# The leftover rows of four batches as one more seven-product half batch, and a new order of all steps

## Chip, cores, metric

One NeuronCore of a Trainium2 chip runs the whole kernel; the other cores are idle. The metric is the device time of one execution in microseconds, taken as the median of three timed runs.

## What is computed

Packed attention followed by a feed-forward block, all float32. With batch 8, 8 heads, 576 tokens, head width 64, and 32 packed queries per head:

```python
p_packed = sm_attn(p, k, v)
out = sm_attn(q, p_packed, p_packed)
...
h = x @ w_in
g = h * (1.0 / (1.0 + np.exp(-h)))
return (g @ w_out).astype(np.float32)
```

`x` is the attention output of all 4608 tokens with the heads side by side (512 wide); `w_in` is 512 x 2048, `w_out` 2048 x 512. `sm_attn` is a softmax attention with the scale 1/8.

## The kernel before

Precision: each big product of float32 values is made of three products of rounded parts, upper by upper, upper by lower and lower by upper (`todo` in `terms`, lines 669 to 675). An upper half is a cast on ScalarE, a lower half a subtraction on VectorE.

Work is done batch by batch. The attention of a batch ends in weights of the packed tokens (`a2`), and `w_in` is multiplied into the packed tokens once per batch (`Packs`, steps `pp`, `pu`, `pl`), a quarter of the 2048 hidden features at a time. A *unit* then makes hidden values for some features of a batch and multiplies them with `w_out`:

- Batches 0 and 1 (the early units 0 to 31): step `h` makes one block of 128 features for all 576 tokens in `ps_two` (line 615), `g` and `l` the SiLU and its halves, `o` the products with `w_out` into `ps_acc` (line 673, 12 matmuls of 512 columns). Meanwhile `w_in` and `w_out`, which arrive as float64, are converted by ScalarE, VectorE and GpSimd (steps `wf` to `wl`), and sums of `w_out` blocks are made and kept in DRAM (`r`, `R`, `ru`, `rl`, `rk`, `T`).
- Batches 2 to 7: a unit is a half batch (256 of its 288 tokens, `MAIN`) and a pair of feature blocks. `B` makes the hidden values (12 matmuls of 288 columns), `G` their SiLU into tile `g`, `I` three sums on GpSimd (`pair_sums`, lines 644 to 649), `F` and `L` the upper and lower halves of seven 128 x 128 blocks (lines 657 to 667), `O` the products (`pair_products`, lines 716 to 737): Strassen's form with seven block products in place of eight, 21 matmuls of 256 columns into four accumulators. Three of the seven need sums of `w_out` blocks, which `S` loads for each unit from DRAM (768 KB). After 8 pairs `E` (`pair_rows`) adds the accumulators up and stores a half batch.
- Each half batch leaves 32 tokens, 64 per batch. `N` puts their SiLU values into the tile `rest`. For two batches at a time these 128 rows are a *rest* unit of four feature blocks: `F`, `L` on 512 columns of `rest`, and `O` is `rest_products` (lines 705 to 712), 12 matmuls of 512 columns in the plain form. There are 16 rest units: 32 to 35 (batches 0 and 1), 68 to 71, 104 to 107 and 140 to 143, the last of the kernel. `Y` (`rest_rows`) stores them.

Between early and later units stand `Z0.` and `Z1.`: they give the memory of `win` (all of `w_in`) and of the early accumulators to others. From then on a quarter of `w_in` is fetched from DRAM (`pf`, 1024 KB, into the single buffer `w_quarter`) before its `pp`.

The order on TensorE, VectorE, ScalarE and SyncE is the order of the steps in the table `ORDER`, as written; only GpSimd's is left to the scheduler. SyncE issues nearly all DMAs, in that order, and a DMA that waits holds those behind it. `g`, `g_hi` and `g_lo` have two buffers each, `ps_two` two, the four accumulators one.

Of the kernel before, what the change touches and what calls it, by code (L numbers as in the profile page):

```python
# [66 lines left out]
pl5 aH1.1 aL1.1 o6 o7 e7.0 h8 g8 r0 e7.1 wf14 l8 wc12 h9 as2.1 o8 g9 ws13 ac2.1 h10 am2 wz12 h11 l9 g10 wc13 v2 pp6 R0
wi12 wj12 wf15 l10 ru0 rl0 wz13 o9 o10 rk0 r1 R1 ax2.0 ax2.1 g11 l11 pu6 at2.0 o11 q2 pl6 h12 h14 wi13 ws14 g12 h13
at2.1 wc14 ws15 wj13 wf17 l12 o12 T0 wz14 ay2 wi14 g13 l13 o13 wc15 wz15 wi15 g14 l14 pp7 h15 ru1 rl1 pu7 pl7 wj14 r2
wj15 wu15 wl15 o14 h16 g15 ws17 l15 wf16 h17 wc17 rk1 g16 wz17 l16 wu14 wl14 o15 e15.0 g17 e15.1 wi17 wj17 wf18 h18  # L70
l17 o16 ws16 wc16 ar2 R2 wz16 wi16 h19 g18 l18 o17 wj16 pp8 ru2 rl2 g19 l19 aa2 pu8 r3 o18 ws18 pl8 b0 an2 wc18 h20
o19 wz18 ai2 wi18 g20 l20 wj18 wu18 h21 wf19 ws19 aj2 R3 rk2 wl18 wc19 wz19 wi19 wj19 g21 pp9 pu9 l21 pl9 o20 x2 h22
g22 l22 o21 wu19 wl19 h23 aS2.1 ru3 rl3 o22 x3 g23 aT2.1 l23 T1 r4 R4 rk3 x0 X0 X1 x1 aM2.1 aN2.1 h24 X0 T3 o23 g24
l24 h25 h26 e23.0 ru4 rl4 rk4 e23.1 g25 l25 r5 o24 pp10 g26 l26 aS2.0 o25 aT2.0 pu10 pl10 aX2.1 h27 aM2.0 aN2.0 aX2.0
aD2.0 X1 b1 aE2.0 T2 h28 k3 o26 R5 ru5 rl5 rk5 T5 g27 l27 h29 T4 aV2.0 aH2.0 g28 r6 R6 l28 o27 g29 l29 o28 h31 aD2.1
aL2.0 h30 ru6 rl6 rk6 T6 r7 o29 g30 R7 l30 aE2.1 aV2.1 v3 g31 o30 aH2.1 ru7 X0 l31 rl7 o31 rk7 e31.0 e31.1 pp11 Z0.
# [870 lines left out]
```

## Time and profile before

| | us |
|---|---|
| median of 3 runs | 680.04 (679.95 to 680.74) |
| profiled execution, its own time | 681.22 |
| its span | 679.4 |
| TensorE busy in the span | 660.8 |
| VectorE busy | 428.9 |
| ScalarE busy | 423.3 |
| GpSimd busy | 229.1 |

Times in the profile count from the start of the span; what lies around the span (681.22 - 679.4 = 1.8 us) is not in it. A matmul's row shows its latency, so that busy time of TensorE covers short gaps; the pace of a run of matmuls is the length of that run over its count. The granted clock was 1.0 of 2.4 GHz all along after the first microseconds.

### The profile page before, as it was taken

What the parts mean: (1) busy time and instruction counts of PE and PEld (TensorE: products, weight loads), DVE (VectorE), ACT (ScalarE), POOL (GpSimd) and SP (SyncE); (2) the same over time, 40 slices, a digit from 0 to 9 for tenths busy, and PEclk for the clock granted to TensorE, in tenths of its full rate; (3) what the DMA queues carried; (4) which work ended last, traced back from release to release, by engine and by line L of the source; (5) the groups of instructions that cost most, each with busy time, mean ns of one, the idle gap of its engine ahead of it and who ended that gap; (6) DMA issues with size and microseconds to landing.
All of it is one profiled execution on the core that took longest, in us unless ns stands there. A gap on an engine that the chain in (4) does not pass through costs nothing.

```text
span 679.4 us, 14828 instructions
## 1 busy us (share of the span) xinstructions
PE 660.8 (97%) x5980; PEld 584.2 (86%) x5980; DVE 428.9 (63%) x595; ACT 423.3 (62%) x706; POOL 229.1 (34%) x337
## 2 busy tenths in 40 slices
PE   8898999999999999999999999999999999999997
PEld 6676778787878998899888998899988999899995
DVE  4999999987784356653576428763567426663433
ACT  4798876757557456764466638684367644766442
POOL 1111213243222543444242533445341343444440
PEclk9999999999999999999999999999999999999999
DMA  9748284968688669877798477977889278767441
GB/s 360 321 158 332 71 325 121 335 232 328 241 317 311 226 264 371 330 291 268 269 354 312 132 293 274 368 272 270 325 299 363 81 263 302 247 251 259 166 171 46
DMA packets 55107, 178.62 MB, mean 263 GB/s; under 512 B 21760, under 2 KB 25856, under 8 KB 47360
## 3 DMA queue, kind: packets, MB, share of 16 engines
q1 hardware_dynamic: 54944, 177.56, 70.9%
q8 instruction: 47, 0.77, 0.4%
q10 hardware_dynamic: 96, 0.13, 0.1%
q14 instruction: 20, 0.16, 0.1%
HBM read 149.42 MB, written 24.12 MB: 255 GB/s over the span
## 4 chain that ended last, share of the span: by engine, by line
PE 72%; DVE 9%; ACT 8%; DMA 4%; issue 4%; SPq 2%; POOL 1%; ACTq 0%; DVEq 0%; POOLq 0%
PE ps_acc L673 42%; PE ps_two L615 23%; PE ps_two L304 6%; DMA win<-in_w_out 2%; DVE g_lo L633 2%; SPq L388 2%; DMA sums_of_w<-sums_of_w 1%; ACT g_hi L663 1%; DVE g_lo L667 1%; DVE o L815 1%; PE ps_two L408 1%; ACT g L626 1%; DMA w_raw<-in_w_out 1%; ACT L188 1%; ACT g_hi L627 1%
## 5 line engine op out<-in xcount | busy, mean ns | idle before, releaser
L667 DVE TENSOR_TENSOR g_lo<-g,g_hi 128x896 fp32r<-128x896 f32 x96 | 108.5, 1134 | 132.5 <-ACT g_hi L663 129.7
L673 PE MATMUL ps_acc<-wo_hi,g_hi 128*128 128x256 f32 (+1 forms) x576 | 183.0, 318 | 0.7 <-DVE o L815 0.7
L673 PE MATMUL ps_acc<-wo_hi,g_lo 128*128 128x256 f32 (+1 forms) x576 | 182.1, 316 | 0.7 <-DVE g_lo L633 0.6
L673 PE MATMUL ps_acc<-wo_lo,g_hi 128*128 128x256 f32 (+1 forms) x576 | 181.4, 315 | 0.0
L615 PE MATMUL ps_two<-a_hi,pw_hi 128*128 128x288 f32 x512 | 152.0, 297 | 0.8 <-ACT tm L331 0.3
L615 PE MATMUL ps_two<-a_hi,pw_lo 128*128 128x288 f32 x512 | 150.9, 295 | 0.0
L615 PE MATMUL ps_two<-a_lo,pw_hi 128*128 128x288 f32 x512 | 150.6, 294 | 0.2 <-DVE a_lo L546 0.2
L647 POOL TENSOR_TENSOR g<-g 128x128 f32<-128x128 f32 x96 | 51.8, 540 | 273.1 <-ACT g L637 241.1
L663 ACT CAST g_hi<-g 128x896 fp32r<-128x896 f32 x96 | 90.0, 941 | 77.0 <-POOL g L649 40.6
L673 PEld LDWEIGHTS ps_acc<-wo_hi,g_hi 128*128 128x128 f32 x576 | 108.2, 188 | 14.8 <-issue 6.9
L673 PEld LDWEIGHTS ps_acc<-wo_hi,g_lo 128*128 128x128 f32 x576 | 108.3, 188 | 10.2 <-DVE g_lo L633 2.4
L673 PE MATMUL ps_acc<-sums_of_w,g_hi 128*128 128x256 f32 x576 | 115.6, 282 | 1.0 <-DMA sums_of_w<-sums_of_w 1.0
L673 PEld LDWEIGHTS ps_acc<-wo_lo,g_hi 128*128 128x128 f32 x576 | 108.2, 188 | 6.6 <-DVE wo_lo L297 0.3
L615 PEld LDWEIGHTS ps_two<-a_hi,pw_hi 128*128 128x128 f32 x512 | 96.3, 188 | 7.1 <-issue 3.0
L673 PEld LDWEIGHTS ps_acc<-sums_of_w,g_hi 128*128 128x128 f32 x576 | 87.8, 188 | 15.0 <-issue 13.3
L615 PEld LDWEIGHTS ps_two<-a_lo,pw_hi 128*128 128x128 f32 x512 | 96.4, 188 | 1.4 <-DVE a_lo L546 0.4
L615 PEld LDWEIGHTS ps_two<-a_hi,pw_lo 128*128 128x128 f32 x512 | 96.2, 188 | 0.0
L637 ACT ACTIVATE g<-ps_two 128x512 f32<-128x512 f32 x96 | 57.1, 598 | 42.9 <-PE ps_two L615 22.7
L673 PE MATMUL ps_acc<-sums_of_w,g_lo 128*128 128x256 f32 x288 | 80.0, 278 | 0.0
L648 POOL TENSOR_TENSOR g<-g 128x256 f32<-128x256 f32 x96 | 73.1, 763 | 6.5
L649 POOL TENSOR_TENSOR g<-g 128x128 f32<-128x128 f32 x96 | 56.7, 592 | 6.5
L673 PEld LDWEIGHTS ps_acc<-sums_of_w,g_lo 128*128 128x128 f32 x288 | 54.2, 188 | 0.4 <-DVE g_lo L667 0.4
(131 smaller groups left out, 838.1 us busy)
## 6 DMA issues: line engine op xcount, KB each, us to landing
sums_of_w<-sums_of_w SPq DMA_DIRECT2D x96, 768.0 KB, 6.4
w_quarter<-w_in SPq DMA_DIRECT2D x22, 1024.0 KB, 7.2
kvq_t<-in_v SPq DMA_DIRECT2D x8, 1280.0 KB, 9.3
kvq_t<-in_pkT SPq DMA_DIRECT2D x7, 1216.0 KB, 10.4
out<-o SPq DMA_DIRECT2D x16, 512.0 KB, 3.6
kvq_t<-in_qT SPq DMA_DIRECT2D x7, 1152.0 KB, 8.4
w_raw<-in_w_in SPq DMA_DIRECT2D x6, 1024.0 KB, 8.1
sums_of_w<-w_sums SPq DMA_DIRECT2D x8, 768.0 KB, 4.6
```

The costliest lines, as they stand in the source:

```text
L188: nc.scalar.activation(ready, ident[:, :1], (AF.Exp, AF.Silu)[n])
L304: nc.tensor.matmul(bank(par)[NP * i : NP * i + NP], lhs(r, i), rhs(r, i), start=True, stop=True)
L388: nc.sync.dma_start(self.e1T[NP * at : NP * at + NP, : some.shape[1], i], some)
L615: nc.tensor.matmul(bank, p[:, par, cols], a[:, par], start=(n == 0), stop=(n == len(todo) - 1))
L633: nc.vector.tensor_tensor(g_lo[:, c], g[:, c], g_hi[:, c].bitcast(F32), ALU.subtract)
L637: nc.scalar.activation(g[:, : 4 * P].rearrange("p (e s) -> p e s", e=2), made["h", u, None][..., :MAIN], AF.Silu)
L647: nc.gpsimd.tensor_tensor(x[:, 4], x[:, 0], x[:, 2], ALU.subtract)
L648: nc.gpsimd.tensor_tensor(x[:, 5:7], x[:, 0:5:4], one, ALU.subtract)
L649: nc.gpsimd.tensor_tensor(x[:, 7], x[:, 3], x[:, 6], ALU.add)
L663: nc.scalar.copy(both[0], g)
L667: nc.vector.tensor_tensor(g_lo, g, g_hi.bitcast(F32), ALU.subtract)
L673: nc.tensor.matmul(out, g[:, rows], w, start=(first and n == 0), stop=(last and n == 2), skip_group_check=True)
```

## The change

The rest rows of batches 0 to 3, and again of 4 to 7, become 256 rows, a further half batch with eight pair units. `rest` holds two batches; those of the first two are written to DRAM (`D`, `kept_rest`) and read back (`C`, `load_rest`) into a buffer of `kvq`, and `M` (`copy_rest`) puts both together in a tile `g` with two ScalarE copies. `I`, `F`, `L`, `O` then follow as for any pair; in the last eight units `I` runs on VectorE. Rest units are now 64 to 71 and 136 to 143, with no `B`, `G` or `N`. The pairs of every second half batch are taken as 4 to 7, 0 to 3, so that four tiles of sums stay from one half to the next: `S` falls from 96 to 76. The last unit puts its bank-2 products last, and the stores of the last rest half are eight DMAs, four on each of two queues, in place of four.

```diff
-PACKS += [(b, j * FJ, FJ) for b in range(EARLY, B) for j in range(NJ)]
+PACKS += [(b, j * FJ, FJ) for b in range(EARLY, B) for j in ((0, 1, 2, 3), (2, 3, 0, 1))[b % 2]]
+PAIRS = (0, 1, 2, 3, 4, 5, 6, 7), (4, 5, 6, 7, 0, 1, 2, 3)
...
-L40 B42 G42 X1 O39 S40 O40 N41 F41 N42 ay3.1 B43 N43 I42 F42 L41 S41 aa3 G43 O41 X0 an3 L42 ai3 aj3 B44 S42 N44 G44
...
+ay3.1 F38 L38 B40 N40 G40 B41 aa3 N41 I39 an3 S38 F39 L39 G41 T6 O38 S39 T7 ai3 B42 q3 I40 aj3 O39 pf15 F40 L40 G42 I41
...
-    units += [(0, f, "rest") for f in range(0, NF, FJ)]
     for b in range(EARLY, B):
-        units += [(b, (hf, p)) for hf in range(2) for p in range(NPAIR)]
-        if b % 2:
-            units += [(b - 1, f, "rest") for f in range(0, NF, FJ)]
+        units += [(b, (hf, p)) for hf in range(2) for p in PAIRS[(b + hf) % 2]]
+        if b % 4 == 3:
+            units += [(b - 3, ("rest", p)) for p in PAIRS[1]]
...
-        nc.gpsimd.tensor_tensor(x[:, 4], x[:, 0], x[:, 2], ALU.subtract)
-        nc.gpsimd.tensor_tensor(x[:, 5:7], x[:, 0:5:4], one, ALU.subtract)
-        nc.gpsimd.tensor_tensor(x[:, 7], x[:, 3], x[:, 6], ALU.add)
+        engine = nc.vector if units[u][0] == B - 4 and units[u][1][0] == "rest" else nc.gpsimd
+        engine.tensor_tensor(x[:, 4], x[:, 0], x[:, 2], ALU.subtract)
+        engine.tensor_tensor(x[:, 5:7], x[:, 0:5:4], one, ALU.subtract)
+        engine.tensor_tensor(x[:, 7], x[:, 3], x[:, 6], ALU.add)
+
+    def keep_rest(j):
+        nc.sync.dma_start(kept_rest[j], rest[:, FJ * j : FJ * j + FJ].rearrange("p f e h s -> p (f e h s)"))
+
+    def load_rest(n):
+        t = in_turn(kvq, [P, 5 * DM], F32, "kvq_t")[:, : NF * P]
+        nc.sync.dma_start(t.rearrange("p (j x) -> p j x", j=NJ), kept_rest.rearrange("j p x -> p j x"))
+        made["rest", n] = t.rearrange("p (f s) -> p f s", s=P)
+
+    def copy_rest(u):
+        b, (_, p) = units[u]
+        g = hidden[u] = in_turn(gp_main, [P, 8 * P], F32, "g")
+        g = g[:, : 4 * P].rearrange("p (e r s) -> p r e s", e=2, r=2)
+        nc.scalar.copy(g[:, 0], made["rest", b // 4][:, 2 * p : 2 * p + 2])
+        nc.scalar.copy(g[:, 1], rest[:, 2 * p : 2 * p + 2].rearrange("p f e h s -> p f (e h s)"))
...
-    def rest_products(u):
...
-        x = summed_tiles.pop((b, hf, p))
+        x = summed_tiles[p]
...
-        term(2, low, 6, *w(f2, high))
+        if not final:
+            term(2, low, 6, *w(f2, high))
         term(3, low, 1, *t(1))
         term(3, high, 3, *w(f1, high))
+        if final:
+            term(2, low, 6, *w(f2, high))
...
-        x = summed_tiles[b, hf, p] = in_turn(tp, [P, 2, 3 * HALF], F32R, "sums_of_w", TP_BUFS)
+        x = summed_tiles[p] = tp.tile([P, 2, 3 * HALF], F32R, name="sums_of_w", tag=f"sums_of_w_{p % TP_BUFS}", bufs=1)
...
+    def rest_rows(n):
+        o = pair_rows(n, "rest", n == 1)
+        for k in range(2):
+            for m in range(4):
+                at = (4 * n + 2 * k) * S + m * HS + MAIN
+                (nc.scalar if n and m % 2 else nc.sync).dma_start(out[at : at + REST], o[m * REST : m * REST + REST, k])
```

Three places of the new order follow, as rows of one engine each (line, operation, tile written <- tiles read, size, count).

SyncE, where early units end and the rest begins; `out` are the stores of the last early half batches. Before:

```order
L794 DMA out<-o 128x2x512 x2
L556 DMA w_quarter<-w_in_114 128x2048
L744 DMA sums_of_w<-sums_of_w 128x1536
L777 DMA wo_hi<-first_sums 128x256
L777 DMA wo_lo<-first_sums 128x256
L744 DMA sums_of_w<-sums_of_w 128x1536 x3
L556 DMA w_quarter<-w_in_114 128x2048
```

Now:

```order
L653 DMA kept_rest<-rest 128x512
L783 DMA wo_hi<-first_sums 128x256
L783 DMA wo_lo<-first_sums 128x256
L799 DMA out<-o 128x2x512 x2
L558 DMA w_quarter<-w_in_115 128x2048
L750 DMA sums_of_w<-sums_of_w 128x1536 x3
L558 DMA w_quarter<-w_in_115 128x2048
```

The first quarter (`pf13`) still stands right behind the two stores.

TensorE at the same place, from the last matmul of the early `o31` to the first `pp` on a fetched quarter (`pp13`); the rows between, left out, are the further matmuls of the same kinds. Before:

```order
L673 MATMUL ps_acc<-wo_hi,g_lo 128x512
L304 MATMUL ps_two<-win,ppT 32x512 x16
L673 MATMUL ps_acc_2221<-wo_hi,g_hi 128x512
...
L304 MATMUL ps_two<-kvq_t 32x288 x16
...
L615 MATMUL ps_two<-a_hi,pw_hi 128x288
...
L304 MATMUL ps_two<-w_quarter,ppT 32x512 x8
```

Now:

```order
L684 MATMUL ps_acc<-wo_hi,g_lo 128x512
L306 MATMUL ps_two<-kvq_t 32x288 x8
L306 MATMUL ps_two<-win,ppT 32x512 x8
L615 MATMUL ps_two<-a_hi,pw_hi 128x288
...
L306 MATMUL ps_two<-kvq_t 32x288 x8
L306 MATMUL ps_two<-w_quarter,ppT 32x512 x8
```

Before, three rest units (`O32` to `O34`) and two `B` stand between; now only `as3.0`, `pp12`, `B32`, `B33` and `as3.1`.

VectorE from the last main units into the last rest units; `o<-ps_acc` are the five additions of `E7.1`. Before:

```order
L667 TENSOR_TENSOR g_lo<-g,g_hi 128x896 x7
L667 TENSOR_TENSOR g_lo<-rest,g_hi 128x512
L815 TENSOR_TENSOR o<-ps_acc_2222,o 128x2x256
L815 TENSOR_TENSOR o<-ps_acc_2221,o 128x256
L815 TENSOR_TENSOR o<-ps_acc_2224,o 128x256
L815 TENSOR_TENSOR o<-ps_acc_2223,o 128x256
L815 TENSOR_TENSOR o<-ps_acc_2224,o 128x512
L667 TENSOR_TENSOR g_lo<-rest,g_hi 128x512 x3
```

Now:

```order
L648 TENSOR_TENSOR g<-g 128x128
L649 TENSOR_TENSOR g<-g 128x256
L650 TENSOR_TENSOR g<-g 128x128
L678 TENSOR_TENSOR g_lo<-g,g_hi 128x896
L806 TENSOR_TENSOR o<-ps_acc_2280,o 128x2x256
L806 TENSOR_TENSOR o<-ps_acc_2279,o 128x256
L806 TENSOR_TENSOR o<-ps_acc_2282,o 128x256
L806 TENSOR_TENSOR o<-ps_acc_2281,o 128x256
L806 TENSOR_TENSOR o<-ps_acc_2282,o 128x512
L678 TENSOR_TENSOR g_lo<-g,g_hi 128x896
```

Two `I` (136 and 137) and `L136` now stand ahead of the five additions, and of each later unit VectorE gets three sums and a lower half of 896 columns.

## Rows read from the trace of the kernel before

**Rows 1.** The page's busy times of the engines over the span.
```profile
PE 660.8 (97%) x5980; PEld 584.2 (86%) x5980; DVE 428.9 (63%) x595; ACT 423.3 (62%) x706; POOL 229.1 (34%) x337
```

**Rows 2.** Busy time by stretch: PE, PEld, DVE, ACT, POOL, clock, DMA share, GB/s.
```profile
20.00:140.00 120.00, 112.05 (x944) 88.06 (x943) 113.81 (x161) 94.65 (x162) 29.61 (x24) 1.00 0.65 236
195.00:217.00 22.00, 22.00 (x176) 16.13 (x176) 13.85 (x18) 13.71 (x22) 3.27 (x6) 1.00 0.98 371
217.00:660.00 443.00, 440.38 (x4223) 408.33 (x4223) 241.88 (x329) 262.62 (x435) 176.51 (x282) 1.00 0.74 270
```

**Rows 3.** What TensorE waited for: us in total, times, longest.
```profile
PE ps_acc L673 <- DMA sums_of_w<-sums_of_w: 1.0, 1, 1.0
```

**Rows 4.** The chain that ended last, in order of time: start us, us, what.
```profile
187.70 8.19 PE ps_acc L673 x36
195.89 1.88 PE ps_two L304 x32
...
290.75 4.78 PE ps_acc L673 x42
...
488.88 6.34 PE ps_two L615 x48
...
518.98 10.90 PE ps_acc L673 x48
```

**Rows 5.** Timeline of SyncE's DMA issues at 195 to 200: start us, us.
```profile
196.05 1.88 SPq L794 DMA_DIRECT2D out<-o  x2
197.98 1.17 SPq L556 DMA_DIRECT2D w_quarter<-w_in  x1
```

**Rows 6.** The tile w_quarter: its 22 loads, from issue to landing.
```profile
DMA to landing us min/median/max: 4.7/7.2/11.7
```

**Rows 7.** Timeline of TensorE at 195.5 to 212: scores, and the first fetched quarter.
```profile
200.64 1.20 PE L304 MATMUL ps_two<-kvq_t 64*32 64x288 f32 x32
210.60 1.09 PE L304 MATMUL ps_two<-w_quarter,ppT 64*32 64x512 f32 x16
```

**Rows 8.** Groups by form: line, engine, op, tiles, shapes, count | busy, mean ns | idle before.
```profile
L667 DVE TENSOR_TENSOR g_lo<-g,g_hi 128x896 fp32r<-128x896 f32 x96 | 108.5, 1134 | 132.5 <-ACT g_hi L663 129.7 <-PE ps_two L615 2.5
L663 ACT CAST g_hi<-g 128x896 fp32r<-128x896 f32 x96 | 90.0, 941 | 77.0 <-POOL g L649 40.6 <-PE ps_acc L673 35.1 <-DVE tm L364 0.7
L581 DVE TENSOR_TENSOR pw_lo<-ps_two,pw_hi 128x1024 fp32r<-128x1024 f32 x31 | 37.6, 1215 | 22.8 <-ACT pw_hi L578 22.4
L578 ACT CAST pw_hi<-ps_two 128x1024 fp32r<-128x1024 f32 x31 | 31.4, 1017 | 18.5 <-PE ps_two L304 18.5
L667 DVE TENSOR_TENSOR g_lo<-rest,g_hi 128x512 fp32r<-128x512 f32 x16 | 10.9, 683 | 10.3 <-ACT g_hi L663 10.3
L816 ACT COPY o<-ps_acc 128x256 f32<-128x256 f32 x12 | 4.5, 371 | 8.6 <-PE ps_acc L673 8.6
L800 DVE TENSOR_TENSOR o<-o 128x256 f32<-128x256 f32 x4 | 1.6, 412 | 3.5 <-ACT o L799 3.5
```

**Rows 9.** Timeline at 655 to 680, around the last `E` and the first last rest unit.
```profile
662.14 0.28 PE L673 MATMUL ps_acc<-sums_of_w,g_lo 128*128 128x256 f32 x1
...
662.46 0.37 ACT L816 COPY o<-ps_acc 128x256 f32<-128x256 f32 x1 [0.91 <-PE ps_acc L673]
...
662.87 2.60 DVE L815 TENSOR_TENSOR o<-ps_acc,o 128x512 f32<-128x512 f32 x5 [0.59 <-ACT o L816]
...
663.20 0.28 PE L673 MATMUL ps_acc<-wo_hi,g_lo 128*128 128x256 f32 x1
...
664.23 0.47 PE L673 MATMUL ps_acc<-wo_hi,g_hi 128*128 128x512 f32 x1 [0.75 <-DVE o L815]
```

**Rows 10.** Timeline at 674.9 to 679.4, the end.
```profile
675.03 0.39 PE L673 MATMUL ps_acc<-wo_hi,g_lo 128*128 128x512 f32 x1
675.46 0.69 DVE L801 TENSOR_TENSOR o<-ps_acc,o 128x512 f32<-128x512 f32 x1 [0.31 <-PE ps_acc L673]
676.18 0.81 SPq L808 DMA_DIRECT2D out<-o  x2
676.18 0.87 ACTq L808 DMA_DIRECT2D out<-o  x2
```

More of the change, by code (lines that the diff above doesn't have):

```diff
@@ L67 @@
[L67 to L76, printed above, removed]
@@ new lines @@
+e31.0 ac3.0 e31.1 pp12 pu12 pl12 B32 N32 Z0. G32 I32 B33 Z1. pf13 N33 as3.1 ac3.1 G33 S34 F32 L32 pp13 pu13 pl13 B34
+I33 F33 L33 N34 S32 B35 S33 pf14 O32 G34 I34 B36 am3 ax3.0 ax3.1 ar3 F34 O33 at3.0 at3.1 N36 L34 S35 S36 O34 N35 G35
+G36 pp14 I35 F35 pu14 B37 L35 G37 I36 O35 F36 ay3.0 X1 N37 pl14 I37 B38 F37 L36 N38 S37 B39 G38 N39 L37 O36 O37 G39 I38
+ay3.1 F38 L38 B40 N40 G40 B41 aa3 N41 I39 an3 S38 F39 L39 G41 T6 O38 S39 T7 ai3 B42 q3 I40 aj3 O39 pf15 F40 L40 G42 I41
+E2.0 B43 F41 L41 N42 O40 I42 N43 aS3.0 aT3.0 G43 aM3.0 pp15 I43 F42 aS3.1 pf16 pu15 aT3.1 O41 pl15 L42 aM3.1 B44 k4 F43
@@ new lines @@
+G127 I127 S127 I126 aL7.1 F126 L126 B129 S126 O125 F127 B128 N128 N129 G128 I128 O126 L127 O127 G129 E7.0 B130 F128
+L128 G130 B131 I129 I130 N130 O128 F129 L129 G131 I131 F130 B133 N133 N131 O129 B132 F131 L130 O130 L131 G132 I132 N132
+S132 G133 I133 F132 L132 O131 B134 B135 F133 L133 G134 O132 S133 O133 N135 G135 S134 I134 X1 I135 F134 L134 F135 L135
+O134 M136 I136 M137 I137 F136 L136 S135 O135 E7.1 N134 M138 F137 L137 O136 M139 I138 I139 O137 F138 L138 F139 L139 O138
+M140 I140 F140 S140 L140 M141 I141 S141 M142 I142 O139 F141 L141 O140 O141 F142 L142 M143 I143 S142 X0 S143 F143 L143
@@ L123 @@
+O142 O143 Y1
 """
@@ L703, in packed_attention_ffn @@
     low, high = slice(0, HALF), slice(HALF, DM)
-    def rest_products(u):
-        b, f, _ = units[u]
-        first, last = f == 0, f + FJ == NF
-        for n in sorted(range(FJ), key=lambda n: n % 2) if last else range(FJ):
-            bank = 0 if n % 2 == 0 and (f + n) // 2 in summed else 2
-            begun = opened.get(("rest", b, bank))
-            opened["rest", b, bank] = True
-            products(acc[bank], u, f + n, n, not begun, last and n >= FJ - 2)
     opened = {}
@@ L718, in pair_products @@
         g_hi, g_lo = hidden[u][-2:]
-        last = p == NPAIR - 1
+        last = is_last(u)
+        final = last and u == len(units) - 1
         def term(bank, cols, at, w_hi, w_lo):
-            key = "pair", b, hf, bank
+            key = b, hf, bank
             begun = opened.get(key)
@@ L794, in store, with pair_rows @@
         nc.sync.dma_start(out[at : at + MAIN].rearrange("(k p) e -> p k e", p=P), o)
-    def rest_rows(b):
-        o = in_turn(osb, [P, 2, DM], F32, "o")
-        if opened.get(("rest", b, 0)):
-            nc.scalar.copy(o[:, 1], acc[0])
-            nc.vector.tensor_tensor(o[:, 1, high], o[:, 1, high], o[:, 1, low], ALU.add)
-            nc.vector.tensor_tensor(o[:, 0], acc[2], o[:, 1], ALU.add)
-        else:
-            nc.scalar.copy(o[:, 0, low], acc[2][:, low])
-            nc.vector.tensor_copy(o[:, 0, high], acc[2][:, high])
-        for n in range(4):
-            at = b * S + n * HS + MAIN
-            rows = slice(n * REST, n * REST + REST)
-            (nc.scalar if n % 2 and b == B - 2 else nc.sync).dma_start(out[at : at + REST], o[rows, 0])
-    def pair_rows(b, hf):
+    def pair_rows(b, hf, final=False):
         o = in_turn(osb, [P, 2, DM], F32, "o")
@@ L867, in packed_attention_ffn @@
         "L": all_lower,
-        "O": lambda u: (rest_products if len(units[u]) > 2 else pair_products)(u),
-        "E": pair_rows,
+        "O": pair_products,
+        "E": main_rows,
+        "C": load_rest,
+        "M": copy_rest,
+        "D": keep_rest,
         "Y": rest_rows,
```

135 lines of the change are left out of this document (68 added, 67 removed).

## Prediction, made before the change was run

> **What bounds the kernel now.** I read the busy times first, then stretches, the chain in order of time, and the timelines at the places where the order changes.
>
> TensorE is busy 660.8 of 679.4 us [rows 1]. From 217 to 660, where batches 2 to 7 run, it is idle 443 - 440.38 = 2.6 us in all [rows 2]; its waits for sums of `w_out` are 1.0 us of that [rows 3]. So this stretch is as long as its matmuls, and work taken from TensorE there is won in full, while better loads there can win 2.6 us at most. In 20 to 140 it is idle 8 us, and VectorE is busy 113.81 of 120 us [rows 2]: there the conversion of weights on VectorE is the limit. The seam between early and later units, 195 to 217, has no idle TensorE at all, with the DMA engines busy 0.98 [rows 2].
>
> **Products.** 16 rest units fewer in the plain form take away 16 x 12 = 192 matmuls of 512 columns; 16 pair units more add 16 x 21 = 336 of 256. In the chain 48 matmuls of 512 columns take 10.90 us, 0.2271 each, and 42 of 256 take 4.78, 0.1138 each [rows 4]. So 192 x 0.2271 = 43.6 go and 336 x 0.1138 = 38.2 come: **-5.4 us**. A matmul of half the width costs half, so nothing is lost by the 144 more instructions. The Trainium skill, TensorE: Matmul & The Clock Gate, section on the 56 ns gap, gives each warm matmul a fixed 2.5 ns on top of its columns; by it the 144 would give back 0.4 us. The two rows show no such part between 512 and 256 columns.
>
> **The seam.** Let T be the end of `o31`, 195.89 before (187.70 + 8.19) [rows 4]. SyncE issues the two stores of the early sums at T + 0.2, and behind them the first quarter of `w_in` at 197.98, T + 2.1 [rows 5]. Quarters land 4.7 to 11.7, median 7.2 us after issue [rows 6]: T + 9.3. Before, `pp13`, which reads it, stands at 210.60, T + 14.7 [rows 7], behind three rest units and two `B`, so nobody waits. The change takes the rest units away. Its TensorE has, from T on: `as3.0` and `as3.1`, half of 1.20 each [rows 7]; `pp12`, half of 1.88 [rows 4]; two `B` of 6.34 / 4 = 1.585 [rows 4]. That is 1.2 + 0.9 + 3.2 = 5.3 us. The load isn't earlier: the two stores stand ahead of it still, and the second waits for VectorE's addition after `o31`. So TensorE waits at `pp13` for 9.3 - 5.3 = 4.0 us. The next pair of `B` adds a little: `B35` needs the `ps_two` buffer of `pp13`, which takes 1.02 + 1.22 = 2.2 us to read out [rows 8] against 1.6 of `B34`: 0.6. Together **+4.6**. The lower end is the fastest landing, 2.1 + 4.7 - 5.3 + 0.6 = +2.1; the upper the slowest, +9.1. I take the median, since three loads of sums follow the quarter at once, as they do before. The Trainium skill, DMA: Bandwidth & Descriptors, section on bandwidth, measures 6.15 us for a lone load of 1 MB issued from GpSimd; by it, as an estimate, the seam would cost 3.5 and the whole sum be 1.1 us lower. The rows' median of 7.2 decides, being this queue under this traffic.
>
> **The last rest half.** Its `I` runs on VectorE. One `I` is two sums of 128 columns and one of 256: 0.41 for 256 [rows 8], and 0.28 for 128, since from 256 to 512 columns the time grows by 683 - 412 = 271 ns [rows 8], so by 0.13 for 128 fewer: about 1.0 together. `L` is 1.13, `F` on ScalarE 0.94 [rows 8], `M` two copies of 0.37 by the nearest row, a copy of 256 columns [rows 8]. From the end of `O134` VectorE must do eight `I`, eight `L` and the five additions of `E7.1`, 2.60 [rows 9]: 8.0 + 9.1 + 2.6 = 19.7 us, while eight `O` of 21 x 0.1138 take TensorE 19.1. VectorE thus has no slack, and it also stands idle, because `F` of a unit needs the `g_hi` buffer of the unit two back, so the end of that `O`. Walking the order with these durations: `L136` stands ahead of the additions, which therefore free the accumulators 1.3 us late for `O136`, and one bank 0.2 later again; `L137`, behind the additions, is 0.5 late; `L138`, behind two `I`, 0.8; `L141`, behind two `I`, 0.6. Sum 3.4. Before, the same place lost from 663.20 + 0.11 to 664.23, 0.9, for the additions [rows 9], and its rest units were not late after. So **+2.4**; between 0 (only the additions cost, as before) and +3.5. The first rest half, 64 to 71, keeps `I` on GpSimd and has other work of TensorE between its products: nothing, unless GpSimd falls behind.
>
> **The end.** Before, the last addition starts 675.46, 0.43 after the start of the last matmul, and the stores issue 1.15 after it [rows 10]. Now all of `pair_rows` follows: the copy starts 0.32 after the twelfth matmul of a unit (662.14 to 662.46) and the five additions end at 662.87 + 2.60 = 665.47, which is 2.27 after the last matmul's start at 663.20 [rows 9]. That is +1.1. Each queue then has four stores instead of two, at 0.41 to 0.43 each [rows 10]; the first two may go while the last addition runs, so one more is seen: +0.4. **+1.5**, between +1.0 and +2.0.
>
> **What costs nothing.** `M`'s 32 copies, `D` and `C`: ScalarE and the DMA engines have room (0.74 busy from 217 on [rows 2]), and the covering work is TensorE's; if `C` were late, `O64` would be. The orders of the start differ much, yet up to the lower half `l19` both give VectorE the same 177 instructions, counted in the orders; as it is the limit there, I expect that stretch to be as long as before, +-1.5 us. The 20 fewer loads of sums can take away some of the 2.6 us of waits from 217 on: -0.5, between -2 and, by new waits where eight small copies of `ay3` stand ahead of sums on SyncE, +2.
>
> **Sum.** -5.4 + 4.6 + 2.4 + 1.5 - 0.5 = +2.6 us. Against the profiled execution's 681.22 that is 683.8. That execution is 1.2 above the median of the runs, so I predict **682.6**. What a measurement can tell from no change is 0.2%, 1.4 us.
>
> **Rivals.**
> *The quarter comes early and the last half flows.* With the fastest landing the seam costs 2.1, with `L` always in time the last half 0.5 (only the additions): -5.4 + 2.1 + 0.5 + 1.5 - 1.0 = -2.3, so 677.7. For it: the two stores before are the only big transfers that must be ahead. Against: the DMA share of 0.98 there. A new order that shortened the stretch limited by VectorE would add to it, to 674 or so; 120 - 113.8 = 6.2 us of idle VectorE is all there is [rows 2], and the equal count speaks against it.
> *The parts cancel.* The quarter lands in 5.6, so the seam costs 3, and the last half loses 1.5: -5.4 + 3 + 1.5 + 1.5 - 0.5 = 0.1, so 680.1.
> *The seam starves.* The quarter takes the slowest 11.7, and the sums behind it, wanted by `O32` to `O34` in the next 10 us, land late as well. +9.1 at the seam in place of 4.6: 687.1. It decides once the landing passes 10 us.
> *The change doesn't save products*: if 256 columns paced like more than 0.130 each, 336 would cost the 43.6 that go; the rows at 0.1138 exclude it.
>
> **Chances.** Forecast, slower by 1.4 to 5 us: 0.44. Seam starving: 0.10. Cancelling: 0.22. The first rival: 0.24. So faster 0.24, within 0.2% 0.22, slower 0.54. The range that leaves out 2 in 10 goes from 676.0, inside the first rival, to 687.0, the starved seam; the likeliest case alone is 681.5 to 685.
>
> **What would show it.** The groups of products: 2352 matmuls of 256 columns at 0.114 and 384 of 512. In the timeline, TensorE idle some 4 us ahead of the first `pp` on `w_quarter`, with the DMA as what ended it; then waits for VectorE in the last eight units, 3 us in all; the span ending about 5.9 us after the last matmul's start, 679.4 - 675.03 = 4.4 before. I'm wrong if `pp13` starts within 2 us of `as3.1`, if the last eight units take 20 us or less, or if the early units end more than 2 us away from 197 (195.9, and half of 1.88 for `pp11`, which now stands ahead of `o31`).

## The result, and the profile of the changed kernel

| | kernel before | changed kernel |
|---|---|---|
| median us | 680.0 (679.59 to 680.74, 4 runs) | 689.69 (689.03 to 690.47, 4 runs) |
| profiled execution, span us | 681.22, 679.4 | 689.41, 687.6 |
| mean granted clock of TensorE | 1.000 | 0.987 |

The ratio is 1.0142, with a 95% interval of 1.0124 to 1.0159: slower by 9.7 us, where 2.6 was forecast and 687.0 was the range's end. The two profiled executions differ by less, 8.2 us: that of the kernel before is 1.2 above its median, that of the changed kernel 0.3 below.

The busy times of the page, which answer to [rows 1]:

```profile
PE 660.8 (96%) x6124; PEld 592.0 (86%) x6124; DVE 436.9 (64%) x621; ACT 435.5 (63%) x735; POOL 245.7 (36%) x361
```

TensorE's sum is the same, although its products take 5.5 us less: a matmul at half clock counts as busy for longer, and so do short gaps between matmuls. The stretches of [rows 2] (same columns) show where it stood idle: 3.3 us in the seam, 6.1 from 217 to 660.

```profile
20.00:140.00 120.00, 114.38 (x937) 89.95 (x937) 110.94 (x162) 95.02 (x164) 27.27 (x22) 0.96 0.66 240
195.00:217.00 22.00, 18.68 (x169) 14.82 (x168) 12.98 (x16) 13.82 (x22) 6.26 (x9) 1.00 0.97 379
217.00:660.00 443.00, 436.94 (x4279) 408.98 (x4277) 245.28 (x334) 265.75 (x450) 189.75 (x303) 1.00 0.64 234
```

TensorE's waits (us in total, times, longest), where [rows 3] had one of 1.0 for sums:

```profile
PE ps_two L306 <- DMA w_quarter<-w_in: 4.0, 2, 2.0
PE ps_acc L482 <- DVE tm L532: 2.6, 1, 2.6
PE ps_acc L684 <- DVE g_lo L633: 2.4, 1, 2.4
...
PE ps_two L615 <- DVE pw_lo L583: 1.4, 3, 0.6
...
PE ps_acc L684 <- DVE o L806: 1.2, 1, 1.2
PE ps_two L306 <- ACT rest L641: 1.1, 1, 1.1
PE ps_acc L684 <- DVE g_lo L678: 0.9, 2, 0.5
```

One of the two quarters is the seam's. The other is pack 25's: in SyncE's timeline its fetch stands behind the load of `v` and behind a load of sums that waits for the products of `O83`, and TensorE's timeline has the wait.

```profile
425.97 0.33 SPq L238 DMA_DIRECT2D kvq_t<-in_v  x1
429.08 0.32 SPq L750 DMA_DIRECT2D sums_of_w<-sums_of_w  x1
429.49 0.38 SPq L558 DMA_DIRECT2D w_quarter<-w_in  x1
```
```profile
437.27 0.72 PE L306 MATMUL ps_two<-kvq_t 64*32 64x288 f32 x16
439.93 1.09 PE L306 MATMUL ps_two<-w_quarter,ppT 64*32 64x512 f32 x16 [1.94 <-DMA w_quarter<-w_in]
```

Behind this wait the clock (the number ahead of the DMA share) falls to its lower level, 1.2 of 2.4 GHz, for 3.4 us:

```profile
436.00:437.50 1.50, 1.50 (x20) 1.33 (x27) 0.00 (x0) 1.50 (x3) 0.66 (x2) 1.00 0.98 350
441.00:444.40 3.40, 3.40 (x31) 2.62 (x13) 2.13 (x3) 3.25 (x4) 0.00 (x0) 0.51 0.69 242
445.00:448.00 3.00, 3.00 (x26) 3.00 (x25) 2.93 (x6) 1.95 (x4) 0.01 (x1) 1.00 0.58 169
```

The same follows the waits of 2.6 and 2.4 us for VectorE at 25 and 38 us: 10.2 us at half clock between 28 and 45. The trace of the kernel before has no stretch at half clock ahead of its last products, and behind its first matmuls no wait above 1.4:

```profile
PE ps_two L304 <- ACT ident L188: 1.4, 1, 1.4
```

**Where the 8.2 us of span went.** Below, each stretch runs from the end of one unit's products to that of another, read off TensorE's timeline. "Matmuls" is their count times the spacing of undisturbed ones in the kernel before (0.113 us for 256 columns, 0.227 for 512, 0.132 for 288, the small ones by their mean). The other rows are the time over that: waits, and what half clock adds. The last two columns are kernels of the experiments.

| us | before | changed | q25 | front_loads |
|---|---|---|---|---|
| matmuls, and 1.7 ahead of the first | 637.5 | 632.0 | 632.0 | 632.0 |
| to the end of `o31` | 20.3 | 22.0 | 19.9 | 23.7 |
| seam: four units behind `o31` | 0.9 | 5.0 | 5.8 | 2.5 |
| to `O79` | 7.7 | 5.6 | 5.6 | 5.5 |
| `O79` to `O95` | 2.3 | 6.8 | 3.6 | 3.6 |
| `O95` to `O111` | 2.3 | 4.3 | 3.4 | 3.8 |
| `O111` to the last products | 4.0 | 5.4 | 5.4 | 5.6 |
| last matmul's start to the end | 4.4 | 6.6 | 6.5 | 6.6 |

The products gave 5.5. The seam took 4.1, `O79` to `O95` 4.5, `O95` to `O111` 2.0, the start 1.7, the last stretch 1.4, the end 2.2; up to `O79` 2.1 came back, where there are fewer waits.

### The profile page after: what moved, and what is told of

Same layout as the page of the kernel before. It is cut to its first block, busy times and chain, and to the rows that moved or that the text cites. A ratio compares the mean times of both kernels' runs of the same rounds, so it can differ in the third digit from the quotient of the medians.

```text
span 687.6 us, 15202 instructions
## 1 busy us (share of the span) xinstructions
PE 660.8 (96%) x6124; PEld 592.0 (86%) x6124; DVE 436.9 (64%) x621; ACT 435.5 (63%) x735; POOL 245.7 (36%) x361
## 4 chain that ended last, share of the span: by engine, by line
PE 83%; DVE 9%; ACT 3%; DMA 2%; issue 2%; POOL 0%; SPq 0%; DVEq 0%; ACTq 0%; POOLq 0%
PE ps_acc L684 46%; PE ps_two L615 26%; PE ps_two L306 6%; DMA w_quarter<-w_in 2%; PE ps_two L213 2%; PE ps_two L410 1%; DVE g_lo L678 1%; ACT g_hi L674 1%; DVE g_lo L633 1%; DVE win L287 1%; DVE o L806 1%; DVE pw_lo L583 1%; DVE w_raw L275 1%; DVE win L283 1%; DVE w_raw L271 1%
## 5 line engine op out<-in xcount | busy, mean ns | idle before, releaser
L678 DVE TENSOR_TENSOR g_lo<-g,g_hi 128x896 fp32r<-128x896 f32 x112 | 126.2, 1132 | 135.8 <-ACT g_hi L674 135.6
L684 PE MATMUL ps_acc<-wo_hi,g_lo 128*128 128x256 f32 (+1 forms) x576 | 175.1, 304 | 2.4 <-DVE g_lo L633 2.4
L684 PE MATMUL ps_acc<-wo_hi,g_hi 128*128 128x256 f32 (+1 forms) x576 | 175.8, 305 | 0.0
L674 ACT CAST g_hi<-g 128x896 fp32r<-128x896 f32 x112 | 105.2, 942 | 78.0 <-POOL g L650 40.1
L648 POOL TENSOR_TENSOR g<-g 128x128 f32<-128x128 f32 x104 | 57.0, 548 | 253.3 <-ACT g L637 241.7
L684 PE MATMUL ps_acc<-sums_of_w,g_hi 128*128 128x256 f32 x672 | 135.2, 283 | 1.2 <-DVE o L806 1.2
L684 PEld LDWEIGHTS ps_acc<-sums_of_w,g_hi 128*128 128x128 f32 x672 | 102.9, 189 | 15.0 <-issue 8.6
L684 PE MATMUL ps_acc<-sums_of_w,g_lo 128*128 128x256 f32 x336 | 93.6, 279 | 1.0 <-DVE g_lo L678 0.9
L649 POOL TENSOR_TENSOR g<-g 128x256 f32<-128x256 f32 x104 | 80.4, 774 | 6.6
L684 PEld LDWEIGHTS ps_acc<-sums_of_w,g_lo 128*128 128x128 f32 x336 | 63.4, 189 | 1.6 <-DVE g_lo L678 1.6
L650 POOL TENSOR_TENSOR g<-g 128x128 f32<-128x128 f32 x104 | 61.1, 589 | 6.6
```

Of the source, the lines that this page charges most:

```text
L648: engine.tensor_tensor(x[:, 4], x[:, 0], x[:, 2], ALU.subtract)
L649: engine.tensor_tensor(x[:, 5:7], x[:, 0:5:4], one, ALU.subtract)
L650: engine.tensor_tensor(x[:, 7], x[:, 3], x[:, 6], ALU.add)
L674: nc.scalar.copy(both[0], g)
L678: nc.vector.tensor_tensor(g_lo, g, g_hi.bitcast(F32), ALU.subtract)
L684: nc.tensor.matmul(out, g[:, rows], w, start=(first and n == 0), stop=(last and n == 2), skip_group_check=True)
```

## Experiments

Ratios are to the kernel before, with their 95% intervals. `q25` and what is built on it include pack 25's early fetch.

### One step of SyncE: q25 and quarters

```diff
- pp24 pu24 v6 O83 B86 G86 S87 aM5.1 pl24 pf25
+ pp24 pf25 pu24 v6 O83 B86 G86 S87 aM5.1 pl24
```

> The changed kernel with one step moved: the fetch of pack 25's quarter stands right behind pp24, ahead of the load of v and of the sums that wait for a product. Theory waits-and-clock: the 2.3 us wait at pp25 goes and with it the 1.5 us that TensorE loses in 3.4 us at half clock behind it; the stretch from O79 to O95 (76.8 us) takes 73.5, the time is 686.2. Rival: the wait goes, yet the time is given back behind it, because the load of v and the sums now land later: 689 to 690.

684.64 us (682.33 to 687.21), ratio 1.0068 (1.0051 to 1.0086): 5.1 less than the changed kernel. Against `O79`'s end the fetch is issued 2.6 us earlier, lands in 6.1 us instead of 10.3, and has landed 4.8 before it is used; `O79` to `O95` takes 73.7 and the clock stays full there. Nothing was given back behind it. So in the profiled executions one order in a queue cost 3.1 of the 8.2 us: 1.9 for the wait, the rest for the half clock.

That is the most that any trace shows. `seam`, `early_quarter`, `start` and `sums_pool` below keep the changed kernel's order at this place. In their traces the quarter landed in 8.9 to 9.7 us, TensorE waited 0.5, 1.0, 0.8 and 1.4 for it, the clock stayed full there, and the stretch took 74.4 to 75.2: 0.7 to 1.5 more than with the step moved. `pp25` in `seam`, then in `early_quarter`:

```profile
439.28 1.09 PE L305 MATMUL ps_two<-w_quarter,ppT 64*32 64x512 f32 x16 [0.54 <-DMA w_quarter<-w_in]
438.30 1.09 PE L305 MATMUL ps_two<-w_quarter,ppT 64*32 64x512 f32 x16 [0.98 <-DMA w_quarter<-w_in]
```

What makes up the rest of the 5.1 between the medians is not shown. q25's profiled execution also kept its full clock at the start, which is not of this edit, and lost it for 3.4 us in the seam:

```profile
20.00:140.00 120.00, 112.67 (x947) 89.27 (x947) 111.48 (x162) 97.24 (x169) 29.43 (x24) 1.00 0.68 248
```

With the same steps and waits of 2.6 and 2.3 us there, `o31` ends at 196.2 instead of 198.3. So the 10.2 us at half clock cost the changed kernel 2.1 us.

`quarters` had the same edit, and `pp29` and `pp30` behind `O102` and `O104`:

> The changed kernel with the fetch of pack 25's quarter moved to right behind pp24 (ahead of the load of v and of the sums that wait for a product), and pp29 and pp30 moved behind O102 and O104. Theory waits-and-clock: the 2.0 us wait at pp25, the 1.2 us wait at pp29 and the 3.4 us at half clock behind pp25 (1.4 us lost) all go: 689.7 - 4.6 = 685.1 us, and the granted clock stays full between 45 and 660 us. Theory waits alone: if the half clock doesn't hang on that wait it stays, 689.7 - 3.2 = 686.5. Rival: the waits are only where a general lack (transfers, late VectorE) shows, and turn up elsewhere: 689 or more.

692.20 us (690.75 to 694.27), ratio 1.0166 (1.0152 to 1.0180). `O79` to `O95` took 73.6 as hoped, but with `pp29` and `pp30` moved `O95` to `O111` took 82.5 instead of 76.4, 3.4 us of it at half clock behind this wait:

```profile
PE ps_two L614 <- ACT g L636: 3.7, 1, 3.7
```

### The clock: fill25 and warm_q25

> The changed kernel with 18 matmuls of 128 columns on the unit matrix put in front of pp25's, 2.0 us of work in the time in which TensorE waits for the quarter; nothing else is moved. Theory clock: the wait as such stays (pp25 still starts when the quarter lands), but the granted clock doesn't fall behind it and the stretch from O79 to O95 is 1.5 us shorter, 75.3 instead of 76.8: 688.2. Rival: the clock falls for another reason, and the 3.4 us at half clock stay: 689.7, or more by what the 18 stand past the landing.

691.79 us (690.47 to 692.96), ratio 1.0167 (1.0154 to 1.0180). I had sized it wrong: each of the 18 is two passes of 0.112 us, so the fill took 4.2 us and ended 3.3 after the quarter's landing. TensorE came to `pp25` 2.3 us later than with the bare wait (4.2 against 1.9), yet the stretch is only 1.1 longer (77.9): 1.2 is what the full clock gave back. By itself this run doesn't show that the fill kept the clock, since it also stayed full here behind the shorter bare waits of the four kernels named above. The clock behind the fill:

```profile
445.00:448.40 3.40, 3.40 (x50) 2.45 (x35) 1.40 (x2) 2.42 (x3) 0.00 (x0) 1.00 0.36 104
```

`warm_q25` does it at three places at once:

```diff
- aD0.1 wc5 W2 aU0.0
+ aD0.1 wc5 W12 aU0.0
+ for _ in range(9): nc.tensor.matmul(ps[:, 0, :P], ident, ident, start=True, stop=True)   # ahead of h1.0, and of pp13
```

> q25 (the changed kernel with pack 25's quarter fetched ahead of v), with matmuls on the unit matrix put where TensorE waits longest: ten more ahead of aU0.0 (2.2 us), nine ahead of h1.0 and nine of pp13 (2.0 us each, each of the nine being two passes of 0.112). They add work and take no wait away. Theory clock: the waits of 2.3 to 2.7 us are what lets the granted clock fall, and that costs the changed kernel 4 to 5 us in most of its executions; with TensorE busy there it stays full, and all executions lie where q25's best lay: 682 to 683, with clocks of 0.996 or more (the end alone takes 0.003). Rival: the clock falls for something else, the 28 matmuls only add: 685 to 688 with clocks of 0.988 to 0.995 as in q25.

683.43 us (681.83 to 685.30), ratio 1.0048 (1.0034 to 1.0062). All six executions had clocks of 0.997 or 0.998, where q25's had 0.988 to 0.998 (687.21 at 0.988, 684.36 at 0.991, 684.16 at 0.995, 682.33 at 0.998). So 6.3 us more of matmuls did not make it slower; that its median is 1.2 lower is within the intervals. `mend1` below has the two fills of the start and 0.997 to 0.999 in all seven executions, while of the 18 of q25, light_seam and front_loads, without these fills, three had 0.998 and the others 0.988 to 0.995. (`mend3` and `mend4` have the fills too; their traces have half clock only at the end, which is long there.) That work in TensorE's waits keeps the clock up is thus shown. Between the best and the worst execution, 0.010 of mean clock went with 4.9 us in q25, 4.7 in light_seam and 2.8 in front_loads, so the changed kernel's 0.987 to 0.990 cost it some 2 to 5 us, by estimate.

### The seam: seam, early_quarter, start, start_quarters

```diff
- L32 pp13 pu13 pl13 B34 I33 F33 L33 N34 S32 B35 S33 pf14 O32 G34 I34 B36
+ L32 B34 I33 F33 L33 N34 S32 B35 G34 pp13 pu13 pl13 S33 pf14 O32 I34 N35 G35 B36
```

> The changed kernel with pp13 moved behind B34 and B35 (and G34, N35, G35 moved up so that the two ps_two buffers come free). Theory waits: TensorE's 2.0 us before pp13 and two waits of 0.6 and 0.6 for ps_two and pw_lo are covered by B34 and B35 (3.2 us of work): 689.7 - 2.0 = 687.7, with -3.0 at most. Rival: the quarter only sets when pack 13 is there, the sums for O32 and the quarter share the DMA engines, and the wait moves to O32 or pp14: 689.7 within 0.5.

688.97 us (687.32 to 690.15), ratio 1.0121 (1.0106 to 1.0136). The stretch took 27.8 us, as before the edit (27.7): four waits of 0.6 to 0.7, one of them for sums, took the place. The rival holds in that the wait moved; the 0.7 between the medians is within the intervals.

`early_quarter` puts `pp12` ahead of `o31` and `pf13` ahead of the early stores:

> The changed kernel with pp12 ahead of o31, and the first quarter of w_in fetched as soon as pp12 has read the kept weights, ahead of the two stores of early sums on SyncE. Theory issue: at the seam the quarter is late because it is issued at o31's end plus 1.9 us; issued some 5 us earlier it has landed when pp13 comes, and the stretch from o31 to O35 (27.7 us) loses its 2.4 us: 25.3, the time 687.3. Rival transfers: the DMA engines are the limit there (0.96 busy), the wait turns up at the sums that O32 to O34 read, and the stretch stays at 27 to 28: 689.7.

689.06 us (685.79 to 690.49), ratio 1.0122 (1.0104 to 1.0141). The stretch took 28.6 us, in part at half clock. Nobody waits for the quarter any more; `O32` waits for sums, whose loads stand behind the two stores:

```profile
PE ps_acc L683 <- DMA sums_of_w<-sums_of_w: 2.3, 1, 2.3
```
```profile
194.95 0.33 SPq L557 DMA_DIRECT2D w_quarter<-w_in  x1
...
198.08 1.52 SPq L798 DMA_DIRECT2D out<-o  x2
199.65 2.33 SPq L749 DMA_DIRECT2D sums_of_w<-sums_of_w  x3
```

`start` has the steps up to `o31` in the order of the kernel before; `start_quarters` adds the edits of `early_quarter` and `q25`.

> The changed kernel with the steps up to o31 in the order of the kernel before (with D0 to D2 and pack 11 put in), and everything behind o31 as changed. Theory start: the two waits of 2.7 and 2.6 us for VectorE at 25 and 38 us and the 10 us at half clock are of the new start, and o31 ends 1.5 us earlier (198.3 now, 195.9 before plus 0.95 for pp11): 688.2 us, clock full up to the seam. Rival VectorE: that stretch is bound by VectorE's 177 instructions whatever the order, and o31 ends at 198.3 within 0.5: 689.7. Rival seam: the seam's wait for the quarter grows by what the start gives: 689.7 too, but with o31 earlier.

> The three repairs together: the steps up to o31 in the order of the kernel before, the first quarter issued early, pack 25's quarter ahead of v. If each gives what its rows say: o31 ends 1.8 us earlier, the seam takes 25.3 instead of 27.7, the stretch from O79 to O95 73.5 instead of 76.8: 689.7 - 1.8 - 2.4 - 3.3 = 682.2. If the seam is limited by its transfers, it gives back what the start wins, as the run with the start alone showed: 686.4. Under 680 nothing is expected: what then stays against the kernel before is the stretch O95 to O111 (+2.0), the last half (+1.4) and the end (+2.2), against products of -5.5.

690.03 us (688.44 to 690.70), ratio 1.0135 (1.0121 to 1.0149), and 690.06 (688.99 to 692.98), ratio 1.0151 (1.0133 to 1.0169). In `start` the clock stays full until the seam and `o31` ends 1.8 us earlier, but the seam takes 31.3 us: the two stores and the quarter behind them are issued later against `o31`'s end (the quarter 3.5 us behind it, 1.8 in the changed kernel), it lands 0.2 ahead of `pp13`, whose wait grows to 4.1 us, with 6.8 at half clock behind it. The seam gave back all of it. In `start_quarters` `o31`, now behind `pp12` and a wait of 2.1 us for `l31`'s lower half, ends at 200.8; the seam takes 28.6, with waits of 1.6 for the quarter and 2.8 for sums. So neither the 682.2 nor the 686.4 came.

### Transfers in another order: light_seam, front_loads, covered, early28

> q25 with two transfers moved behind the seam: D3 (a store of 0.26 MB) and T4 (two loads of 0.13 MB each) stand behind pf14 instead of ahead of the early stores. Theory transfers: the seam is limited by what the DMA engines (0.96 busy) must move before the quarter and the sums; 0.5 MB less at 370 GB/s is 1.4 us, the stretch from o31 to O35 takes 27 instead of 28.5: 683.3. Rival issue: the quarter goes out when pp12 and the two stores are done, nothing ahead of them counts: 684.6 within 0.5.

684.93 us (683.22 to 687.95), ratio 1.0073 (1.0052 to 1.0094). The wait for the quarter shrank from 2.0 to 1.4 and the stretch took 27.0 instead of 28.5, but q25's seam also had 3.4 us at half clock, and the time did not fall against q25.

```diff
- g31 l31 o31 D3 aL2.1 T4 X0 as3.0 e31.0 ac3.0 e31.1 pp12 pu12 pl12 B32 N32 Z0. G32
+ g31 l31 pp12 pu12 pl12 o31 Z0. Z2. pf13 S32 S33 S34 aL2.1 X0 as3.0 e31.0 ac3.0 e31.1 B32 N32 G32
...
- S32 B35 S33 pf14 O32
+ B35 pf14 D3 T4 O32
```

(`Z2.` opens the pools of quarters and sums as soon as the kept weights are read; `Z1.` did so before.)

> q25 with pp12 ahead of o31 and, as soon as it is done, the first quarter and the sums of units 32, 33 and 34 fetched on SyncE ahead of the early stores; D3 and T4 behind pf14. Theory order: the seam's loads land late because the two stores of early sums (1 MB), which nobody waits for, and D3 and T4 go first; with the loads in front neither pp13 nor O32 waits, and the stretch from o31 to O35 has 2 us over its matmuls instead of 5 to 6: 684.6 - 3 = 681.6. Theory sum of bytes: 7.7 MB must pass in 19 us at 366 GB/s whatever the order, and what is late next (S35, pf14) takes the wait: 684.6 within 1.

683.91 us (682.41 to 685.18), ratio 1.0047 (1.0035 to 1.0059). The seam has 2.5 us over its matmuls instead of 5.0 to 5.8, and no wait for a transfer is left:

```profile
PE ps_two L614 <- DVE pw_lo L582: 1.0, 1, 1.0
PE ps_two L305 <- ACT g L636: 0.2, 1, 0.2
```
```profile
198.97 0.33 SPq L557 DMA_DIRECT2D w_quarter<-w_in  x1
199.34 1.74 SPq L749 DMA_DIRECT2D sums_of_w<-sums_of_w  x3
202.26 1.52 SPq L798 DMA_DIRECT2D out<-o  x2
```

The bytes are the same, so in the seam their order decided, not their sum. The median gained only 0.7 on q25, which is within the intervals; the profiled execution spent 13.7 us at half clock in its start.

`covered` is light_seam with `pp11 pu11 pl11` behind `o31`; `early28` adds `pp28` and `pf29` ahead of `B101`.

> light_seam with pack 11 behind o31, where the kernel before has it: 1.0 us of TensorE's work that needs no load lies in the seam again. Theory cover: what the seam costs is that the plain rest units (10.9 us of products on data that was there) went from it; 1.0 us of such work put back shortens it by 1.0: 682.3 if light_seam gives 683.3. Rival transfers: o31 ends 1.0 earlier, but the landings don't move with it, and the wait grows: no gain against light_seam.

> covered with pp28 ahead of B101 and pf29 right behind it, 6 us earlier. Theory waits: pp29's wait for its quarter (1.2 us) goes, and pp30's margin grows; the stretch from O95 to O111 takes 74.5 instead of 75.5 to 76.4: 1.0 less than covered. Rival: pp28 in front of B101 takes a ps_two buffer that G99 or G100 frees late, and TensorE waits there instead: no gain.

692.05 us (690.69 to 694.90), ratio 1.0181 (1.0160 to 1.0203), and 692.17 (691.20 to 693.21), ratio 1.0176 (1.0162 to 1.0190). With `pp11` and `pp12` side by side the second waits for the buffer that the first's halves are read from. VectorE's additions for the two stores come behind the first's lower half, and the quarter, behind the stores, is issued 6.9 us behind `o31`'s end, so it comes later still. In early28 `O95` to `O111` took 77.4 us, not 74.5. With the order unchanged there the traces have 75.4 to 77.8 (covered), so this edit's effect is not told apart from that spread. The waits of covered:

```profile
PE ps_two L305 <- DMA w_quarter<-w_in: 2.6, 1, 2.6
PE ps_two L305 <- DVE pw_lo L582: 1.9, 1, 1.9
```

### What the plain rest units did: no_first_rest

The kernel before without `F`, `L` and `O` of units 32 to 35 and `Y0`.

> The kernel before, without the products and outputs of its first four rest units (F, L, O of 32 to 35 and Y0 are left out; the rows 1 to 64 that they give stay unwritten): 48 matmuls of 512 columns, 10.9 us, go from the seam and nothing else is moved. Theory cover: in the kernel before these products ran while the quarter and the sums came in; without them TensorE waits, and the time falls by only 10.9 - 4 = 7 us, to 673, with waits of 2 us and more for w_quarter or sums behind o31, and half clock behind those. Rival: the seam of the changed kernel is slow by its own order, and the kernel before gives the full 10.9: 669.2.

677.42 us (677.25 to 678.31), ratio 0.9957 (0.9946 to 0.9969). Taking 10.9 us of products away saved 3.0: less even than the theory of cover said. TensorE now waits behind `o31`, although the order is that of the kernel before, and 3.4 us follow at half clock.

```profile
PE ps_two L302 <- DMA w_quarter<-w_in: 3.6, 2, 2.9
PE ps_two L302 <- DVE pw_lo L579: 2.0, 2, 1.6
```

From the end of `o31` to that of `O37` the trace has 26.2 us in place of 29.5, so 7.7 of the 10.9 are not won. The waits explain 5.6: 2.9 for the first quarter, 0.7 for the second, 2.0 for the buffers that the halves of `pp11` and `pp12` are read from. The half clock adds some 1.5, where 14 matmuls of `B` follow each other at 0.24 us instead of 0.132. Nothing waits for sums.

So the products that the change takes from this place were worth 3.0 there, and their successors, 16 x 21 x 0.113 / 4 = 9.5 us for four units' share, stand where TensorE hardly waits.

### The last half: sums_pool

```diff
- engine = nc.vector if units[u][0] == B - 4 and units[u][1][0] == "rest" else nc.gpsimd
+ engine = nc.gpsimd
```

> The changed kernel with the I of the last eight units on GpSimd, as everywhere else. Theory last half on VectorE (my forecast's): VectorE has 8.0 us less to do in the last 22.6 us, TensorE no longer waits for L (0.5 + 0.5 and smaller ones): 689.7 - 1.5 = 688.2. Rival: GpSimd takes 1.9 us for an I in place of 1.0, the chain copy, I, F, L of a unit is longer by that and starts only when the g of the unit two back is free: 690 to 692.

691.62 us (688.14 to 693.54), ratio 1.0157 (1.0134 to 1.0180). From the first product of `O136` to the last of all took 24.1 us instead of 21.1, and the waits for the additions and for `L`, 1.2 and 0.9 in the changed kernel, grew to:

```profile
PE ps_acc L684 <- DVE g_lo L678: 1.9, 3, 0.7
PE ps_acc L684 <- DVE o L806: 1.8, 1, 1.8
```

Relieving VectorE doesn't help: in the trace its `L` waits for `F`, up to 2.7 us at a time, and `F` for GpSimd's `I`. So the chain copy, `I`, `F`, `L` of a unit sets the pace, and of the two engines VectorE is the better for `I`.

### Repairs together: mend1 to mend4

> front_loads with pp28 and pf29 earlier (as in early28) and the fills at the start (ten matmuls ahead of aU0.0, nine ahead of h1.0), which keep the clock full there. If order and clock are the causes, the fills give 1.2 as in warm_q25 and pp29's wait 1.0: front_loads - 2, so 679.6 if that gives 681.6, level with the kernel before. Rival: the sum of bytes holds at the seam: 683 to 684.

> The same repairs on the steps of the kernel before up to o31 (no fills; h30 and h31 exchanged, pp11 and pp12 spread over the last early units). Its start has no wait over 2 us and ended 1.7 us earlier in the run of the start alone. If the order of the loads is what held the seam, that 1.7 is kept now: 679 to 680. If the sum of bytes holds it, it is given back: 683 to 685.

> front_loads with the fills at the start, pp28 where the change has it (early28 made O95 to O111 1.4 us longer), and the outputs of a rest half written by two stores of 128 rows, one on each queue, instead of eight of 32 rows. Theory end: the eight issues of 0.43 us, four on a queue, hold the end up by 1.3 us, so the span ends 5.3 us after the last matmul instead of 6.55: 682.8 - 1.4 - 1.3 = 680.1, level with the kernel before. Rival: one store of 256 KB lands later than four small ones by what the issues save, 681.4.

> mend3 with B34 ahead of pp13 and G34 ahead of pu13, so that B35 doesn't take the ps_two buffer that pu13 and pl13 (2.2 us) are still reading. Theory: the 1.0 us wait for pw_lo at B35 goes, and the stretch from o31 to O35 takes 23.4 instead of 24.4: 1.0 less than mend3, 679.1. Rival: B35 waits for G34 and N34 instead, equal to mend3.

mend1: 682.81 us (681.23 to 683.02), ratio 1.0029 (1.0018 to 1.0039), clocks 0.997 to 0.999, the best of the changed form. mend2: 688.91 (688.15 to 690.46), ratio 1.0127 (1.0114 to 1.0140), with a wait of 3.2 us at `pp13` and 6.8 us at half clock. (The profile puts this wait down to ScalarE's `g_hi`, but that ended 0.9 us before; the quarter landed 0.2 before.) mend3: 689.47 (686.12 to 689.81), ratio 1.0121 (1.0100 to 1.0142), and mend4: 687.69 (686.19 to 689.22), ratio 1.0120 (1.0104 to 1.0135). In mend3 the last matmul starts at 673.2, 1.8 earlier than in the kernel before, but the end takes 11.5 us behind it: the two large stores run at a fraction of the DMA engines (tenths of their share in 40 slices from 674 to 690, then GB/s).

```profile
DMA  0000002231122222222222200000000000000000
GB/s 0 0 0 0 0 0 41 15 15 10 46 61 102 102 102 102 102 102 97 102 102 102 87 15 0 0 0 0 0 0 0 0 0 0 0 0 0 0 0 0
```

With the eight small stores' end of 6.6 its span would be 673.2 + 6.6 = 679.8 by estimate, against 679.4 before. mend4's edit moved the wait at `B35` to `G34` (1.7 us). None of the four came to what its theory had (679.6, 679 to 680, 680.1 and 679.1), and no kernel of the changed form that beats the one before was found.

## Why the forecast was wrong, step by step

- **Products -5.4**: right, 5.5. The 0.4 that a fixed part per matmul would give back (the Trainium skill, TensorE: Matmul & The Clock Gate, section on the 56 ns gap) isn't seen: 256 columns stand at 0.113, 512 at 0.227.
- **Seam +4.6**: right in size (4.1), which is in part luck. `pp13` waited 2.0 us, not 4.0: the quarter landed 8.2 us behind `o31`'s end, not 9.3, and TensorE came to it 1.1 later than worked out. Waits for `pw_lo` took 1.3, where 0.6 was counted. The quarter's own landing took 6.45 us, nearer to the Trainium skill's 6.15 (DMA: Bandwidth & Descriptors, section on bandwidth, which leaves the issue out) than to the median of 7.2 that I took. The quarter alone is not the limit, either: issued earlier, it hands the wait to the sums. The loads behind the stores of early sums are, as front_loads shows. And I didn't look at what this load had taken at this very place in the kernel before: 9.0 us, the next one 7.5. With 9.0 the term would have been +6.4.

```profile
DMA to landing us min/median/max: 7.5/8.3/9.0
```

- **217 to 660: -0.5, between -2 and +2**: this step failed. I read 2.6 us of idle TensorE as a property of that stretch, won or lost only by loads of sums. It was one of the old order. The changed order put a quarter behind a load that waits; I counted the queue's order at the seam alone, and never read it at the 21 other quarters. The stretch from the seam to `O111` gave 4.5 + 2.0 - 2.1 = +4.4 in the profiled execution. Of this q25 shows 3.1 to come from pack 25's fetch; what the other 1.4 of `O79` to `O95` and the 2.0 behind `O95` come from no run isolates.
- **The clock**: no term, and this failed too. Behind the new waits TensorE ran at half clock, in this execution for 13.6 us ahead of its last products. Two traces price it: 2.1 us up to `o31` (q25) and 1.2 behind pack 25 (fill25), 3.3 of the 8.2, by estimate; these lie in the terms above and below.
- **Early stretch 0 +-1.5**: `o31` ends at 198.3, within the 2 us around 197, but 1.5 behind the 196.8 worked out. The new order is not what cost it: with the same order and a full clock q25 ends `o31` at 196.2, and `start`, with the old order, at 196.6. That the two orders are worth the same was right; the half clock behind the new waits was left out.
- **Last half +2.4** (its own figures, 3.4 less 0.9, give 2.5): 1.4 measured, waits of 1.2 and 0.9 against 3.4 in all.
- **End +1.5**: 2.2. The additions end 2.3 after the last matmul's start as worked out; the four issues of a queue all come behind the fourth addition, the first 2.0 behind the last matmul's start and the last 3.4, so they and not one more issue end it.

```profile
680.35 0.37 ACT L807 COPY o<-ps_acc 128x256 f32<-128x256 f32 x1 [2.74 <-PE ps_acc L684]
680.76 2.61 DVE L806 TENSOR_TENSOR o<-ps_acc,o 128x512 f32<-128x512 f32 x5 [2.02 <-ACT o L807]
681.06 0.28 PE L684 MATMUL ps_acc<-wo_hi,g_lo 128*128 128x256 f32 x1
683.06 1.75 SPq L828 DMA_DIRECT2D out<-o  x4
```

The sign was right, for reasons that account for about half of it. The rival of the starved seam came nearest in number (687.1), but not in mechanism.

What stays open: why the same wait is followed by half clock in one execution and not in another; where the part of the 5.1 between the medians comes from that q25's trace doesn't show; and the 3.4 us over the matmuls between `O79` and `O111` named above that no run took away.

## What to carry to other kernels

Before counting saved work as won, look at what ran beside it: work on data that is already there may be the cover of a load, and then taking it away gives less than its length (3.0 of 10.9 us here). When an order is rewritten, walk each queue at every fetch that the limiting engine reads, not only at the place that the change is about: a load that waits for a product holds up all behind it. A wait of TensorE can cost more than its length, since the slower clock may follow it (1.9 us of waiting and 1.2 more at pack 25). And a cost read off one trace is that of one execution: the same order cost 3.1 us in one kernel's trace and 0.7 to 1.5 in four others.
